# Values of the last tokens once per block, and attention on pairs of heads, in a memory-augmented recurrent layer

## Chip, cores and metric

The kernel runs on one core of a Trainium2 chip. The metric is the device time of one execution in microseconds; the figure for a kernel is the median of its runs.

## What is computed

Two kinds of layer alternate, twice each, on x of 2048 tokens by 512, every one on a layer norm of x and added to it: A, attention with a recurrent memory, and B, a gated MLP whose gate mixes tokens (the change doesn't touch B). A goes through the tokens in 64 segments of 32, one after the other, because the memory of a segment is the output of the one before:

```python
idx = jnp.arange(L)                       # L = 8 memory rows + 32 tokens
mask = (idx[:, None] < M) | (idx[:, None] >= idx[None, :])
for s in range(n_seg):
    h = jnp.concatenate([mem, xs], axis=1)          # 40 rows of 512
    q, k, v = (einsum('btd,dhe->bhte', h, W) for W in (Wq, Wk, Wv))   # 32 heads of 128
    scores = jnp.where(mask, einsum('bhqe,bhke->bhqk', q, k) * scale, -1e9)
    o = einsum('bhqk,bhke->bhqe', softmax(scores), v)
    o = einsum('bhte,hed->btd', o, Wo)
    mem = o[:, :M, :]
    outs.append(o[:, M:, :])
```

Only the first 8 output rows of a segment are needed by the next one. Inputs and outputs are bf16; matrix products accumulate in f32.

## The kernel before

`a_block` (L345) holds the A layer. The weights stay on chip. The matmul helper `mm_chunk` (L394) computes 32 rows of activations times 2048 columns of weights in one pass: 4 contraction steps by 4 column groups of the PE array, 16 matmuls of 512 columns. Since a pass takes 32 rows and a segment has 40, the rows are split. hA is the memory's 8 rows and the first 24 tokens; it must wait for the segment before. hB is the last 8 tokens of each of four segments (a "block" of 128 tokens), which depend on no memory; they fill 32 rows together.

Q and K of hB are computed once per block, in four passes (`bpass`, L456, one per segment at the end of `segment`, L664), turned by DVE into QTB and KTB, and copied by POOL into the last 8 places of QQ and KK (`prep_segment`, L503). V of the last tokens is not: `v_mm` (L544) makes four passes per segment, and in each, column groups 0 and 2 use hA and groups 1 and 3 use hBs, a zero-padded copy of the segment's own 8 rows (L451), so that a head's 40 keys lie together on partitions 0 to 39 (or 64 to 103) of vs.

A segment goes, in PE's order (L596 to L636): four passes for Q and K (each copied from PSUM by ACT, L538, and turned by DVE, L542), half of V's first pass, `scores(0)`, its other half, `denom(0)`, half of V's second pass, `scores(1)`, the other half, `denom(1)`, V's third pass and half of its fourth, `pv(0)`, the rest, the Wo matmuls of half the heads (`wo_pass`, L467), `pv(1)`, a quarter of the Wo matmuls for the last tokens of the block before (`fill_a`, from `y_pass`, L476), the other half of Wo, and the block pass (`fill_b`). `scores` (L554) is two mask matmuls (an identity times the mask, 320 columns) and 16 matmuls, one for each head of the half, in two column groups of the array; ACT's Exp makes E (L565). `denom` (L567) is one matmul with a block of ones, then Ln and Exp on ACT; `probs` (L575) multiplies on DVE. `pv` (L582) has one matmul for each head, two row groups of the array; ACT copies the 8 memory rows into uT (L589), from which Wo is taken at once, and `tok_out` (L592) copies the rest for the next segment's Wo. `build_hA` (L512) puts the memory rows of the Wo product into the next hA: a predicated copy (L515) and a transpose (L516) on DVE, on which the next segment's first matmul waits.

PE, DVE and ACT work in the order of the program (`manual_schedule`, L369). PSUM has four buffers for passes (`acc`), two for scores and denominators (`att`), one of two banks for PV (`attO`). `_consts` (L52) builds the mask with POOL at the start.

Of the kernel before, what the change touches and what calls it, by code (L numbers as in the profile page):

```python
# [14 lines left out]
P = 128  # L15
# [36 lines left out]
def _consts(ctx, tc):  # L52
# [12 lines left out]
    maskf = cp.tile([P, 40], F32, name="maskf")  # L65
    nc.gpsimd.memset(maskf[:], 0.0)
    for g in range(2):
        blk = maskf[64 * g:64 * g + 64, :]
        nc.gpsimd.affine_select(out=blk[:, 8:40], in_=blk[:, 8:40], compare_op=ALU.is_ge, fill=NEG,
                                base=8, pattern=[[1, 32]], channel_multiplier=-1)  # L70
        nc.gpsimd.affine_select(out=blk[:, 0:8], in_=blk[:, 0:8], compare_op=ALU.is_ge, fill=NEG,
                                base=39, pattern=[[0, 8]], channel_multiplier=-1)
    maskN = cp.tile([P, 40], BF16, name="maskN")
# [270 lines left out]
def a_block(tc, c, xd, MV_in, MV_out, mem0, wqkv, Wo, S):  # L344
# [5 lines left out]
    NHA = 8  # L350

    with ExitStack() as ctx:
# [23 lines left out]
        QK_CH = ([0, 1, 4, 5], [2, 3, 6, 7])  # L376

        def chunk_of(j, cg):
            if j < 2:
                return QK_CH[j][cg]  # L380
            if j < 4:
                return 8 + QK_CH[j - 2][cg]
            return 16 + 4 * (j - 4) + cg

        def wcat(cidx):
            return ((Wq_sb, Wk_sb, Wv_sb)[cidx // 8], (cidx % 8) * 512)

        def qk_rhs(j, kt, cg):
            W_sb = Wq_sb if j < 2 else Wk_sb
            return W_sb[:, kt, :].rearrange("p (g2 s2 i eb el) -> p s2 eb g2 i el", g2=2, s2=2, i=8, eb=4)[:, j % 2, cg]  # L390
# [12 lines left out]
        hBs = [pers.tile([P, KT, 32], BF16, name=f"hBs{i}") for i in range(NHA)]  # L403
        NKQ = 3
        KKr = [pers.tile([P, 2, 16, 40], BF16, name=f"KK{i}") for i in range(NKQ)]
        QQr = [pers.tile([P, 2, 16, 40], BF16, name=f"QQ{i}") for i in range(NKQ)]
        uT = [pers.tile([P, H, 32], BF16, name=f"uT{i}") for i in range(2)]
        for t in uT + hBs:
            nc.gpsimd.memset(t[:], 0.0)
# [37 lines left out]
        def ln_turn(tb):  # L447
            hB = blkp.tile([P, KT, 32], BF16, name="hB")
            nc.vector.transpose(out=hB[:].rearrange("p kt r -> p (kt r)"), in_=blk_state[tb].pop("preB")[:])  # L449
            for j4 in range(4):  # L450
                nc.gpsimd.tensor_copy(hBs[(4 * tb + j4) % NHA][:, :, 0:8], hB[:, :, 8 * j4:8 * j4 + 8])  # L451
            KTB = blkp.tile([P, 2, 16, 32], BF16, name="KTB")
            QTB = blkp.tile([P, 2, 16, 32], BF16, name="QTB")
            blk_state[tb].update(hB=hB, KTB=KTB, QTB=QTB)

        def bpass(tb, j):  # L456
            bs = blk_state[tb]
            ps = acc.tile([P, 512], F32, name="psb")
            mm_chunk(ps, lambda kt, cg: bs["hB"][:, kt, :], lambda kt, cg: qk_rhs(j, kt, cg))
            r = rowp.tile([P, 512], BF16, name="rowsB", bufs=2)  # L460
            nc.scalar.copy(r[:], ps[:])  # L461
            nc.vector.transpose(out=bs[("QTB", "KTB")[j // 2]][:, j % 2].rearrange("p a b -> p (a b)"), in_=r[:])  # L462


        HEADS = [16 * g + 8 * half + i for half in range(2) for g in range(2) for i in range(8)]

        def wo_pass(po, lhs, half=None):  # L467
            for n in range(H) if half is None else range(16 * half, 16 * half + 16):
                h = HEADS[n]
                for cg in range(4):  # L470
                    nc.tensor.matmul(po[32 * cg:32 * cg + 32, 0:128], lhsT=lhs[:, h, :], rhs=wo_rhs(h, cg),  # L471
                                     start=(n == 0), stop=(n == H - 1), tile_position=(0, 32 * cg))
                if n % 8 == 7:
                    yield
# [28 lines left out]
        def prep_segment(s):  # L503
            tb, j4 = s // 4, s % 4
            bs = blk_state[tb]
            KK, QQ = KKr[s % NKQ], QQr[s % NKQ]
# [3 lines left out]
            seg_state[s] = dict(KK=KK, QQ=QQ, vs=vs)  # L510
# [12 lines left out]
        def segment(s, fill_a, fill_b):  # L523
            tb, j4 = s // 4, s % 4
            st = seg_state.pop(s)
            KK, QQ, vs = st["KK"], st["QQ"], st["vs"]
            hA_cur, hB_cur = hA[s % 2], hBs[s % NHA]
# [13 lines left out]
            def qk_T(j, r):  # L541
                nc.vector.transpose(out=(QQ, KK)[j // 2][:, j % 2, :, 0:32], in_=r[:])  # L542

            def v_mm(c, kts, ps=None):  # L544
# [6 lines left out]
            def v_out(c, ps):  # L551
                (nc.vector.tensor_copy if c == 3 else nc.scalar.copy)(vs[:, 4 * c:4 * c + 4, :].rearrange("p h e -> p (h e)"), ps[:])  # L552

            def scores(half):  # L554
                psS = att.tile([P, 8, 40], F32, name="psS")
                for g in range(2):
                    nc.tensor.matmul(psS[64 * g:64 * g + 64], lhsT=ident_bf[:, 64 * g:64 * g + 64],
                                     rhs=maskN[:].unsqueeze(1).to_broadcast([P, 8, 40]),
                                     start=True, stop=True, tile_position=(0, 64 * g), skip_group_check=True)
                for hl in range(8):  # L560
                    for g in range(2):
                        nc.tensor.matmul(psS[64 * g:64 * g + 40, hl, :], lhsT=KK[:, half, 8 * g + hl, :], rhs=QQ[:, half, 8 * g + hl, :],
                                         start=False, stop=True, tile_position=(0, 64 * g), skip_group_check=True)
                E[half] = segp.tile([P, 8, 40], BF16, name="E")
                nc.scalar.activation(out=E[half][:], in_=psS[:], func=ACT.Exp, scale=scale)  # L565

            def denom(half):  # L567
                psD = att.tile([P, 8, 40], F32, name="psD")
                nc.tensor.matmul(psD[:], lhsT=ones64[:], rhs=E[half][:], start=True, stop=True)  # L569
                L = segp.tile([P, 8, 40], F32, name="L")  # L570
                nc.scalar.activation(out=L[:], in_=psD[:], func=ACT.Ln)  # L571
                R[half] = segp.tile([P, 8, 40], BF16, name="R")
                nc.scalar.activation(out=R[half][:], in_=L[:], func=ACT.Exp, scale=-1.0)  # L573

            def probs(half):  # L575
                PT[half] = segp.tile([P, 8, 40], BF16, name="PT")
                nc.vector.tensor_tensor(out=PT[half][:], in0=E[half][:], in1=R[half][:], op=ALU.mult)  # L577

            def hview(t, half, lo, hi):
                return t[:].rearrange("p (g s i) r -> p g s i r", g=2, s=2)[:, :, half, :, lo:hi]  # L580

            def pv(half):  # L582
                psO = attO.tile([P, 2, 512], F32, name="psO")
                for hl in range(8):
                    for g in range(2):
                        nc.tensor.matmul(psO[:, g, 40 * hl:40 * hl + 40], lhsT=vs[64 * g:64 * g + 40, 8 * half + hl, :],  # L586
                                         rhs=PT[half][64 * g:64 * g + 40, hl, :], start=True, stop=True)
                ov = psO[:, :, 0:320].rearrange("p g (h q) -> p g h q", q=40)
                nc.scalar.copy(hview(uT_cur, half, 0, 8), ov[:, :, :, 0:8])  # L589
                return ov  # L590

            def tok_out(half, ov):  # L592
                nc.scalar.copy(hview(uT_nxt, half, 8, 32), ov[:, :, :, 8:32])
                nc.vector.tensor_copy(hview(oB, half, 8 * j4, 8 * j4 + 8), ov[:, :, :, 32:40])
# [8 lines left out]
            v0 = v_mm(0, range(0, 2))  # L603
# [5 lines left out]
            v1 = v_mm(1, range(0, 2))  # L609
            scores(1)  # L610
            v_mm(1, range(2, 4), v1)
            denom(1)
            probs(0)
            v_out(1, v1)
            v2 = v_mm(2, range(KT))
            probs(1)
            v_out(2, v2)
            v3 = v_mm(3, range(0, 2))
            ov0 = pv(0)
            v_mm(3, range(2, 4), v3)  # L620
            v_out(3, v3)
# [5 lines left out]
            fill_a()  # L627
            for _ in wo_pass(pw, uT_cur, 1):
# [5 lines left out]
            tok_out(1, ov1)  # L634
            if s + 1 < NSEG:
# [6 lines left out]
        for j in (0, 2, 1, 3):  # L642
            bpass(0, j)
        build_hA(0, None)
        prep_segment(0)
        for s in range(NSEG):
            tb, j4 = s // 4, s % 4
            if j4 == 0:
# [4 lines left out]
                yp = y_pass(tb - 1) if tb > 0 else iter(())  # L653
            if j4 == 1 and tb + 2 < NB:
# [9 lines left out]
            def fill_b():  # L664
                if tb + 1 < NB:
                    bpass(tb + 1, (0, 2, 1, 3)[j4])
# [3 lines left out]
            segment(s, fill_a, fill_b)  # L670
# [44 lines left out]
```

## Time and profile before

| | us |
|---|---|
| median of 3 runs | 2336.5 (2336.31 to 2343.75) |
| profiled execution | 2348.28 |
| span of it, first to last instruction | 2346.5 |
| PE busy | 2018.0 (86%) |
| ACT busy | 1167.1 (50%) |
| DVE busy | 942.5 (40%) |
| POOL busy | 249.8 (11%) |

Busy times are sums over the span, shares are of the span. Matmuls are pipelined, so that the durations of neighbours overlap, and a busy PE is not one at its peak; what a matmul costs in a row of equal ones is the distance between their starts. A PE whose instructions are late is shown as idle with the releaser "issue". The bracket at the end of a timeline row is the idle time of its engine just before it and what ended it.

### The profile page before, as it was taken

Reading aid. Unit: us, or ns where it says so; the run is one execution under the profiler, and the core shown is the slowest. Engines: PE = TensorE matmul, PEld = TensorE weight load, DVE = VectorE, ACT = ScalarE, POOL = GpSimd, SP = SyncE. Lnnn points to the kernel's source line nnn. Section 1 sums busy time; section 2 is a strip of 40 time slices with the busy share of each in tenths; the row PEclk is TensorE's granted clock in tenths of the full one; section 3 lists DMA queues with packets and bytes.
Section 4 is the critical chain, followed back from the end, with each engine's and each line's share of the span. In section 5 each row is a group of like instructions: output and inputs, shape, how many; then the busy total and the mean of one; then the engine's idle time right before and its main releaser. Section 6 shows DMA issues by size and latency. Waiting matters only on the chain. (4 is left out here: it accounts for less than half of the span.)

```text
span 2346.5 us, 108555 instructions
## 1 busy us (share of the span) xinstructions
PE 2018.0 (86%) x50432; PEld 1146.9 (49%) x50432; DVE 942.5 (40%) x2035; ACT 1167.1 (50%) x2660; POOL 249.8 (11%) x567
## 2 busy tenths in 40 slices
PE   0699998999999999781978999999999999996799
PEld 0345544554554454441754545545545555543476
DVE  2444444444444444250334444444444444442422
ACT  0455655655665555470004655655655555663700
POOL 1100100000110100001220000001100000000022
PEclk9999999999999999885989999999999999998899
DMA  9201111111111110229551011111111111102353
GB/s 363 63 20 32 36 36 32 34 34 32 35 33 32 32 37 22 81 69 259 146 178 28 25 33 34 33 32 33 33 34 35 36 32 32 29 22 91 89 121 100
DMA packets 178692, 145.58 MB, mean 62 GB/s; under 512 B 97472, under 2 KB 148288, under 8 KB 175168
## 3 DMA queue, kind: packets, MB, share of 16 engines
q1 hardware_dynamic: 152544, 83.76, 13.1%
q10 hardware_dynamic: 21728, 30.78, 3.8%
q0 software_dynamic: 3968, 24.12, 2.8%
q8 instruction: 394, 6.46, 1.1%
q14 instruction: 58, 0.48, 0.1%
HBM read 88.13 MB, written 33.70 MB: 52 GB/s over the span
## 5 line engine op out<-in xcount | busy, mean ns | idle before, releaser
L399 PEld LDWEIGHTS <-hA 128*32 128x32 bf16 x12288 | 378.4, 96 | 423.3 <-issue 100.7
L399 PE MATMUL psv<-Wv_sb,hA 128*32 128x512 bf16 x4096 | 580.9, 382 | 0.0
L399 PE MATMUL psv<-Wv_sb,hBs 128*32 128x512 bf16 x4096 | 580.7, 382 | 0.0
L538 ACT CAST rows<-psm 128x512 bf16<-128x512 f32 x512 | 303.3, 593 | 103.7 <-PE psm L399 102.2
L471 PE MATMUL pw<-Wo_sb,uT 128*32 128x128 bf16 x16640 | 292.4, 221 | 61.3 <-issue 57.9
L471 PEld LDWEIGHTS <-uT 128*32 128x32 bf16 x16640 | 241.4, 97 | 114.6 <-issue 67.1
L399 PE MATMUL psm<-Wq_sb,hA 128*32 128x512 bf16 x4096 | 276.7, 382 | 9.4 <-DVE hA L516 7.7
L399 PE MATMUL psm<-Wk_sb,hA 128*32 128x512 bf16 x4096 | 272.3, 380 | 0.0
L461 ACT CAST rowsB<-psb 128x512 bf16<-128x512 f32 x128 | 75.0, 586 | 353.7 <-PE psb L399 353.7
L577 DVE TENSOR_TENSOR PT<-E,R 128x320 bf16<-128x320 bf16 x256 | 83.3, 325 | 403.1 <-ACT R L573 403.1
L208 PE MATMUL pg<-wspT,z2n 128*128 128x256 bf16 (+1 forms) x1536 | 175.1, 275 | 57.9 <-DMA wspT<-in_B_w_sp_dram 57.9
L552 ACT CAST vs<-psv 128x512 bf16<-128x512 f32 x384 | 207.8, 575 | 0.0
L208 PEld LDWEIGHTS <-z2n 128*128 128x128 bf16 (+1 forms) x1536 | 150.5, 100 | 82.3 <-issue 65.3
L542 DVE STREAM_TRANSPOSE QQ<-rows 128x512 bf16<-128x512 bf16 x256 | 179.3, 701 | 27.8 <-ACT rows L538 24.2
L542 DVE STREAM_TRANSPOSE KK<-rows 128x512 bf16<-128x512 bf16 x256 | 178.8, 698 | 21.6 <-ACT rows L538 17.8
L509 POOL COPY QQ<-QTB 128x256 bf16<-128x256 bf16 x128 | 56.4, 456 | 1191.8 <-DVE QTB L462 1002.2
L399 PE MATMUL psb<-Wq_sb,hB 128*32 128x512 bf16 x1024 | 73.1, 394 | 103.1 <-DVE hB L449 73.8
L571 ACT ACTIVATE L<-psD 128x320 f32<-128x320 f32 x256 | 112.0, 437 | 98.1 <-PE psD L569 98.1
L515 DVE CAST_PREDICATED pre<-maskM,pw 128x128 bf16<-128x128 uint16 x126 | 36.7, 291 | 306.8 <-PE pw L471 306.8
L399 PEld LDWEIGHTS <-hBs 128*32 128x32 bf16 x4096 | 156.0, 95 | 1.8
L589 ACT CAST uT<-psO 128x128 bf16<-128x128 f32 x256 | 69.9, 273 | 159.9 <-PE psO L586 159.9
L552 DVE CAST vs<-psv 128x512 bf16<-128x512 f32 x128 | 88.6, 692 | 132.9 <-PE psv L399 132.9
(87 smaller groups left out, 2225.7 us busy)
## 6 DMA issues: line engine op xcount, KB each, us to landing
xs<-xd SPq DMA_DIRECT2D x48, 256.0 KB
xs<-xd ACTq DMA_DIRECT2D x48, 256.0 KB
oA_d<-o_sb SPq DMA_DIRECT2D x130, 64.0 KB
xs_y<-xd SPq DMA_DIRECT2D x32, 256.0 KB
xd<-ot_y SPq DMA_DIRECT2D x32, 256.0 KB
Wq_sb<-in_A_Wq_dram POOLq DMA_DIRECT2D x6, 1024.0 KB, 17.8
Wk_sb<-in_A_Wk_dram POOLq DMA_DIRECT2D x6, 1024.0 KB, 26.2
Wv_sb<-in_A_Wv_dram POOLq DMA_DIRECT2D x6, 1024.0 KB, 20.6
```

The lines of the kernel that those rows point to most:

```text
L208: nc.tensor.matmul(pg[0:fsz, :], lhsT=z2n[:, st_i, f0:f0 + fsz], rhs=wspT[:, st_i, :], start=(st_i == 0), stop=(st_i == NT - 1))
L399: nc.tensor.matmul(ps[32 * cg:32 * cg + 32, :], lhsT=lhs(kt, cg), rhs=rhs(kt, cg), start=(kt == 0), stop=(kt == KT - 1), tile_position=(0, ...
L461: nc.scalar.copy(r[:], ps[:])
L471: nc.tensor.matmul(po[32 * cg:32 * cg + 32, 0:128], lhsT=lhs[:, h, :], rhs=wo_rhs(h, cg), start=(n == 0), stop=(n == H - 1), tile_position ...
L509: nc.gpsimd.tensor_copy(QQ[:, :, :, 32:40], bs["QTB"][:, :, :, 8 * j4:8 * j4 + 8])
L515: nc.vector.copy_predicated(out=t[:], mask=maskM[:], data=pw[:, 0:128])
L538: nc.scalar.copy(r[:], ps[:])
L542: nc.vector.transpose(out=(QQ, KK)[j // 2][:, j % 2, :, 0:32], in_=r[:])
L552: (nc.vector.tensor_copy if c == 3 else nc.scalar.copy)(vs[:, 4 * c:4 * c + 4, :].rearrange("p h e -> p (h e)"), ps[:])
L571: nc.scalar.activation(out=L[:], in_=psD[:], func=ACT.Ln)
L577: nc.vector.tensor_tensor(out=PT[half][:], in0=E[half][:], in1=R[half][:], op=ALU.mult)
L589: nc.scalar.copy(hview(uT_cur, half, 0, 8), ov[:, :, :, 0:8])
```

## The change

V of the last tokens is now computed like their Q and K, once per block: VB, in two further passes, r = 0 and 1. The six passes of a block are made by a generator, `b_units`, in twelve halves; a segment takes one ahead of `pv(0)`, one behind it and one at its end. The copies out of PSUM and DVE's transposes of a finished pass are put off to two calls of `flush` in a segment. hBs and the copies of K are dropped: VA and KA hold the 32 rows of hA alone, KTB and VB the 32 last tokens of all four segments of the block, the other three segments' keys masked out.

Heads are taken in pairs. A score matmul's weights are the keys of two heads (64 columns), its moving side the queries of both; the quarters of the product that mix the heads are masked. So a half has 8 matmuls of 80 columns (32 keys of each head's hA, 40 queries) and 8 of 32 columns (32 keys of the block's last tokens, 16 queries: the 8 last and the 8 memory rows), E has 448 columns instead of 320, and PV has 8 matmuls of 80 and 8 of 32 columns that add up in PSUM. Queries are ordered last tokens, memory, first tokens. Since a query's keys now stand in two column ranges, `denom` and `probs` have two instructions where they had one. Heads are spread over passes and partitions in another order, which `qk_rhs` and `wo_pass` follow.

```diff
-        vs = vsp.tile([P, 16, DH], BF16, name="vs")
-        nc.gpsimd.tensor_copy(KK[:, :, :, 32:40], bs["KTB"][:, :, :, 8 * j4:8 * j4 + 8])
-        nc.gpsimd.tensor_copy(QQ[:, :, :, 32:40], bs["QTB"][:, :, :, 8 * j4:8 * j4 + 8])
+        nc.gpsimd.tensor_copy(QQ[:, :, :, 0:8], bs["QTB"][:, :, :, 8 * j4:8 * j4 + 8])
...
+        def b_units(tb):
+            for j in (0, 2, 1, 3, 4, 5):
+                ps = acc.tile([P, 512], F32, name="psb")
+                for kts in (range(0, 2), range(2, 4)):
+                    mm_chunk(ps, lambda kt, cg: bs["hB"][:, kt, :],
+                             lambda kt, cg: qk_rhs(j, kt, cg) if j < 4 else v_rhs(j - 4, kt, cg), kts)
+                    if kts[0] == 0:
+                        yield
+                def out(j=j, ps=ps):
+                    if j >= 4:
+                        nc.scalar.copy(bs["VB"][:, j - 4].rearrange("p i e -> p (i e)"), ps[:])
+                        return
...
+                copies.append(out)
+                yield
...
-                mm_chunk(ps, lambda kt, cg: (hA_cur if cg % 2 == 0 else hB_cur)[:, kt, :],
-                         lambda kt, cg: Wv_sb[:, kt, 2048 * (cg // 2) + 512 * c:2048 * (cg // 2) + 512 * c + 512], kts)
+                mm_chunk(ps, lambda kt, cg: hA_cur[:, kt, :], lambda kt, cg: v_rhs(r, kt, cg), kts)
...
-                                     rhs=maskN[:].unsqueeze(1).to_broadcast([P, 8, 40]),
+                                     rhs=maskN[:, j4, :].unsqueeze(1).to_broadcast([P, 4, 112]),
...
-                for hl in range(8):
-                    for g in range(2):
-                        nc.tensor.matmul(psS[64 * g:64 * g + 40, hl, :], lhsT=KK[:, half, 8 * g + hl, :], rhs=QQ[:, half, 8 * g + hl, :],
+                for i in range(4):
+                    for K, hi, c0 in ((KA, 40, 0), (KTB, 16, 80)):
+                        for g in range(2):
+                            n = 4 * i + 2 * g
+                            nc.tensor.matmul(psS[64 * g:64 * g + 64, i, c0:c0 + 2 * hi],
+                                             lhsT=K[:, r, n:n + 2, :].rearrange("p h k -> p (h k)"), rhs=QQ[:, r, n:n + 2, 0:hi],
...
+                nc.tensor.matmul(psD[:], lhsT=ones64[:], rhs=E[r][:, :, 0:80], start=True, stop=True, skip_group_check=True)
+                nc.tensor.matmul(dB, lhsT=ones64[:], rhs=eB, start=False, stop=True, skip_group_check=True)
...
             scores(0)
             qk_T(3, r3)
-            v_mm(0, range(2, 4), v0)
+            v0 = v_mm(0, range(KT))
             denom(0)
             v_out(0, v0)
             scores(1)
+            probs(0)
+            v1 = v_mm(1, range(KT))
+            v_out(1, v1)
             denom(1)
+            fill_mid()
+            ov0 = pv(0)
+            fill_mid()
             probs(1)
             tok_out(0, ov0)
...
             ov1 = pv(1)
             fill_a()
+            flush()
...
             fill_b()
             store_o(s, pw)
             tok_out(1, ov1)
+            flush()
```

`v_out` is a DVE copy for both passes (before, ACT's for three of four). The mask, [128, 4, 112] with a plane for each segment of a block, is built by 29 POOL instructions where 5 were.

## Rows read from the trace of the kernel before

**Rows 1.** Windows, first attention stage: us; PE, PEld, DVE, ACT, POOL; clock, DMA, GB/s.

```profile
60.00:1014.00 954.00, 857.16 (x24104) 468.15 (x24105) 403.89 (x855) 539.70 (x1246) 85.51 (x219) 0.98 0.13 39
```

**Rows 2.** Tile hA, DVE's transposes in each of the two blocks: durations, first and last start.

```profile
L516 DVE STREAM_TRANSPOSE hA<-pre x64: 270/312/314, 81.2 to 966.7; 128x128 bf16<-128x128 bf16 x64
...
L516 DVE STREAM_TRANSPOSE hA<-pre x64: 269/312/314, 1246.0 to 2131.8; 128x128 bf16<-128x128 bf16 x64
```

**Rows 3.** Timeline of one segment: start us, us, engine, line, operation, out<-in, count.

```profile
459.13 0.31 DVE L516 STREAM_TRANSPOSE hA<-pre 128x128 bf16<-128x128 bf16 x1
459.50 1.05 PE L399 MATMUL psm<-Wq_sb,hA 128*32 128x512 bf16 x16
...
462.10 1.04 PE L399 MATMUL psm<-Wk_sb,hA 128*32 128x512 bf16 x16
...
462.36 0.66 DVE L542 STREAM_TRANSPOSE KK<-rows 128x512 bf16<-128x512 bf16 x1
...
463.50 0.33 PE L557 MATMUL psS<-maskN,ident_bf 128*64 128x320 bf16 x2
...
463.66 0.36 PE L562 MATMUL psS<-QQ,KK 128*40 128x40 bf16 x16
...
464.06 0.44 ACT L565 ACTIVATE E<-psS 128x320 bf16<-128x320 f32 x1 [0.29 <-PE psS L562]
...
464.55 0.30 PE L569 MATMUL psD<-E,ones 128*128 128x320 bf16 x1
...
464.88 0.44 ACT L571 ACTIVATE L<-psD 128x320 f32<-128x320 f32 x1 [0.38 <-PE psD L569]
...
466.69 0.30 PE L569 MATMUL psD<-E,ones 128*128 128x320 bf16 x1 [0.30 <-ACT E L565]
...
468.32 0.43 PE L586 MATMUL psO<-PT,vs 40*128 40x40 bf16 x16
...
468.81 0.28 ACT L589 CAST uT<-psO 128x128 bf16<-128x128 f32 x1
...
469.14 1.08 PE L471 MATMUL pw<-Wo_sb,uT 128*32 128x128 bf16 x64
...
470.29 0.27 PEld L586 LDWEIGHTS <-vs 40*128 40x128 bf16 x16 [0.25 <-DVE oB L594]
470.30 0.37 PE L586 MATMUL psO<-PT,vs 40*128 40x40 bf16 x16
...
471.06 1.07 PE L471 MATMUL pw<-Wo_sb,uT 128*32 128x128 bf16 x64
471.95 1.04 PE L399 MATMUL psb<-Wk_sb,hB 128*32 128x512 bf16 x16
472.18 0.29 DVE L515 CAST_PREDICATED pre<-maskM,pw 128x128 bf16<-128x128 uint16 x1 [1.93 <-PE pw L471]
```

**Rows 4.** Waits of PE, first attention stage: us in total, times, longest.

```profile
PE pw L471 <- issue: 30.4, 28, 3.8
```

**Rows 5.** The page's DMA queues, the one that brings instructions.

```profile
q8 instruction: 394, 6.46, 1.1%
```

**Rows 6.** Lines by form, 500 to 900 us: busy us, mean ns, idle before.

```profile
L538 ACT CAST rows<-psm 128x512 bf16<-128x512 f32 x116 | 68.8, 594 | 20.9 <-PE psm L399 20.7
...
L562 PE MATMUL psS<-QQ,KK 128*40 128x40 bf16 x912 | 20.6, 180 | 0.0
...
L552 DVE CAST vs<-psv 128x512 bf16<-128x512 f32 x28 | 19.4, 692 | 29.1 <-PE psv L399 29.1
...
L577 DVE TENSOR_TENSOR PT<-E,R 128x320 bf16<-128x320 bf16 x56 | 18.2, 325 | 88.2 <-ACT R L573 88.2
```

**Rows 7.** Timeline of POOL at the start, one of four instructions that cut the mask.

```profile
2.39 0.22 POOL L69 TENSOR_SCALAR_AFFINE_SELECT maskf<-maskf 64x32 f32<-64x32 f32 x1
```

**Rows 8.** Late in the first block: timeline of PE, then the window that follows.

```profile
938.60 1.21 PE L399 MATMUL psm<-Wq_sb,hA 128*32 128x512 bf16 x12 [0.74 <-DVE hA L516]
...
938.90:942.30 3.40, 3.40 (x40) 1.38 (x36) 1.00 (x2) 0.90 (x2) 0.00 (x0) 0.50 0.07 19
```

More of the change, by code (lines that the diff above doesn't have):

```diff
@@ L402, in a_block @@
         hA = [pers.tile([P, KT, 32], BF16, name=f"hA{i}") for i in range(2)]
[L403 removed]
         NKQ = 3
[L405 removed]
+        KAr = [pers.tile([P, 2, 16, 32], BF16, name=f"KA{i}") for i in range(2)]
         QQr = [pers.tile([P, 2, 16, 40], BF16, name=f"QQ{i}") for i in range(NKQ)]
         uT = [pers.tile([P, H, 32], BF16, name=f"uT{i}") for i in range(2)]
[L408 removed]
+        for t in uT:
             nc.gpsimd.memset(t[:], 0.0)
@@ L465, in a_block, with flush @@
-        HEADS = [16 * g + 8 * half + i for half in range(2) for g in range(2) for i in range(8)]
+            VB = blkp.tile([P, 2, 4, DH], BF16, name="VB")
+            blk_state[tb].update(hB=hB, KTB=KTB, QTB=QTB, VB=VB)
+        copies, turns = [], []
+        def flush():
+            while turns:
+                turns.pop(0)()
+            while copies:
+                copies.pop(0)()
+        def b_units(tb):
+            bs = blk_state[tb]
+            for j in (0, 2, 1, 3, 4, 5):
[9 more added lines that the diff above has]
+                        return
+                    r = rowp.tile([P, 512], BF16, name="rowsB", bufs=2)
+                    nc.scalar.copy(r[:], ps[:])
+                    turns.append(lambda: nc.vector.transpose(
+                        out=bs[("QTB", "KTB")[j // 2]][:, j % 2].rearrange("p a b -> p (a b)"), in_=r[:]))
+                copies.append(out)
+                yield
@@ L467, in wo_pass @@
         def wo_pass(po, lhs, half=None):
-            for n in range(H) if half is None else range(16 * half, 16 * half + 16):
-                h = HEADS[n]
+            for h in range(H) if half is None else range(16 * half, 16 * half + 16):
+                n = h // 8 * 8 + 2 * (h % 4) + h // 4 % 2
                 for cg in range(4):
-                    nc.tensor.matmul(po[32 * cg:32 * cg + 32, 0:128], lhsT=lhs[:, h, :], rhs=wo_rhs(h, cg),
-                                     start=(n == 0), stop=(n == H - 1), tile_position=(0, 32 * cg))
-                if n % 8 == 7:
+                    nc.tensor.matmul(po[32 * cg:32 * cg + 32, 0:128], lhsT=lhs[:, n, :], rhs=wo_rhs(h, cg),
+                                     start=(h == 0), stop=(h == H - 1), tile_position=(0, 32 * cg))
+                if h % 8 == 7:
@@ L551, in v_out @@
[L551 to L555, printed above, removed]
+                mm_chunk(ps, lambda kt, cg: hA_cur[:, kt, :], lambda kt, cg: v_rhs(r, kt, cg), kts)
+                return ps
+            def v_out(r, ps):
+                nc.vector.tensor_copy(VA[:, r].rearrange("p i e -> p (i e)"), ps[:])
@@ L575, in probs @@
[L575 to L582, printed above, removed]
-                psO = attO.tile([P, 2, 512], F32, name="psO")
[L584 to L589, printed above, removed]
-                return ov
@@ new lines, in probs, with hview, pv @@
+            def probs(r):
+                PT[r] = segp.tile([P, 4, 112], BF16, name="PT")
+                eB, rB = last(E[r], R[r])
+                nc.vector.tensor_tensor(out=PT[r][:, :, 0:80], in0=E[r][:, :, 0:80], in1=R[r][:], op=ALU.mult)
+                nc.vector.tensor_tensor(out=last(PT[r], R[r])[0], in0=eB, in1=rB, op=ALU.mult)
+            def hview(t, r, lo, hi):
+                return t[:].rearrange("p (r g n) q -> p r g n q", r=2, g=2)[:, r, :, :, lo:hi]
+            def pv(r):
+                psO = attO.tile([P, 2, 512], F32, name="psO")
+                for i in range(4):
+                    for V, c0, c1, nq in ((VA, 0, 80, 40), (VB, 80, 112, 16)):
+                        for g in range(2):
+                            o = psO[:, g, 80 * i:80 * i + 80].rearrange("p (s q) -> p s q", s=2)[:, :, 0:nq]
+                            nc.tensor.matmul(o, lhsT=V[64 * g:64 * g + 64, r, i, :],
+                                             rhs=PT[r][64 * g:64 * g + 64, i, c0:c1].rearrange("p (s q) -> p s q", s=2),
+                                             start=(i == 0 and V is VA), stop=True, skip_group_check=True)
+                ov = psO[:, :, 0:320].rearrange("p g (n q) -> p g n q", q=40)
+                nc.scalar.copy(hview(uT_cur, r, 0, 8), ov[:, :, :, 8:16])
+                return ov
@@ L641, in a_block @@
         ln_turn(0)
-        for j in (0, 2, 1, 3):
-            bpass(0, j)
+        for _ in b_units(0):
+            flush()
+        flush()
         build_hA(0, None)
```

108 lines of the change are left out of this document (47 added, 61 removed).

## The prediction, made before the changed kernel ran

> **What bounds the kernel now.** I read the stages first. Columns of the windows view are busy time of PE, weight loads, DVE, ACT, POOL, then the granted clock. In the first attention stage PE is busy for 857 of 954 us, ACT for 540, DVE for 404 and the DMA queues for an eighth, at a granted clock of 0.98 [rows 1]. So PE sets the time there, and the question is what one segment costs it. The transpose that makes the next hA happens 64 times in each block, from 81.2 to 966.7 us and from 1246.0 to 2131.8 [rows 2]: 63 steps of 14.06 us each time. The two blocks' segments are some 1,771 of the 2,346 us of the span, and the diff touches nothing else that repeats.
>
> Next I read one segment in order of time [rows 3]. It starts on PE at 459.50, and its successor at 472.18 + 0.29 + 0.03 + 0.37 = 472.87 (predicated copy, transpose, the same 0.37 us from hA's transpose to the first matmul as at 459.13): 13.37 us with PE waiting only twice, 0.30 us for E before the second denominator and 0.25 us for the oB copy before the second PV. Everything else follows itself: three projection passes from 459.50 to 462.10, 0.867 us each.
>
> The mean of 14.06 is 0.69 above 13.37. The waits put most of it in the Wo matmuls, with "issue" as the releaser: 30.4 us in 28 waits of the first block [rows 4]. PE's instructions arrive by DMA, 394 packets for 6.46 MB [rows 5], so 16 KB or 256 instructions each, some 2.9 packets a segment (374 matmuls and as many weight loads by the code). Where a packet falls on the Wo matmuls, which use up 64 matmuls in about 0.9 us (471.06 to 471.95), the next packet is late. I read the 0.69 us as that.
>
> **The change, part by part**, for one segment:
>
> V. Four passes with alternating hA and hBs become two with hA alone: 2 x 0.867 = **-1.73 us**. The last tokens' V comes back as two more passes a block. The block's passes are then 6, cut into 12 halves, three a segment: two ahead of and behind the first PV, one at the end. Two halves in the middle cost **+0.87**.
>
> The end. Before, a whole pass (471.95 to 472.87) lies beside the chain from the last Wo matmul to the next hA. Now half a pass, 0.43 us, does. The chain keeps its 0.92 us, so PE idles about 0.48 us there and nothing is gained: **0**.
>
> Masks. Each grows from 320 to 448 columns. At 0.867 / (4 x 512) = 0.42 ns a column and two per segment: **+0.11**.
>
> Scores and PV. The counts stay at 16 matmuls each, but half of them stream 80 columns and half 32, where all streamed 40. The 16 scores take 0.36 us and one has a mean of 0.180 [rows 3, 6], so a pair of column groups follows the next by (0.36 - 0.18) / 7 = 26 ns, above the 17 ns that 40 columns need. A floor of 26 and 80 columns at 0.42 ns make 26 and 34 to 36 ns: four pairs longer by 10 ns in each of two scores and two PVs, **+0.16**. Bounds: 0 (the floor hides it) to +0.32 (see the first rival).
>
> Denominators. A second matmul of 128 columns each; one step of the Wo pass, 128 columns in four groups, is 0.89 / 16 = 0.056 us. Two: **+0.11**.
>
> Waits. A whole V pass now stands between the second scores and the second denominator, where half did, so the 0.30 us wait goes: **-0.30**. The oB copy on DVE had to wait for the fourth V's evacuation (0.69 us, [rows 6]) that was queued ahead of it; now both V evacuations are earlier, and the 0.25 us goes: **-0.25**. What is late next is told below. One change of tile shape fewer: the first mask starts at 463.50, where the third projection's end at 462.10 + 0.867 and half a V pass (0.433) make 463.40, so **-0.10**.
>
> Sum: -1.73 + 0.87 + 0.11 + 0.16 + 0.11 - 0.30 - 0.25 - 0.10 = -1.13, so 12.24 us.
>
> **Does the rest keep up?** From the segment's start, with durations from [rows 3, 6]. QK ends at 3.47. The first K's transpose ended at 462.36 + 0.66, or 3.52, and the first product needs it at 3.57 + 0.21 (mask) = 3.78. Scores to 4.12. E, 448 columns instead of 320: 0.44 us becomes 0.55 (the ACT cost of the 512-column cast, 0.594, and of 320, 0.44, lie 0.8 ns a column apart), until 4.78; the denominator comes after the V pass, at 5.15. Second scores 5.43 to 5.98; E behind Ln and Exp until 6.93; second denominator 7.01: slack under 0.1. First PV at 7.85 needs probabilities from 7.0 (two DVE multiplications, at most 0.33 + 0.33 after 6.47) and V by 5.9. The uT copy (468.81, 0.28 us) is done at 8.65 and the Wo matmuls want it at 8.70: slack under 0.1. An open half-done pass holds one PSUM buffer of four across every second segment boundary, and the Wo pass of the last block another; two remain for the QK passes. One is filled in 0.867 us, copied 0.2 us later in 0.59: 1.7 us against two passes, 1.73: slack under 0.1 again. I charge **+0.05** for these three, bounds 0 to +0.4.
>
> ACT loses three V copies and gains half a row copy, DVE gains one V copy and two small products: neither is near its limit in the [rows 1] shares. POOL's copies of K and hB fall away; nobody waited for them. The constants take 24 more POOL instructions of about 0.2 us [rows 7], 5 us under weight loads that last far longer; cost 0, and 5 us if that cover is gone. Two more passes ahead of each block's first segment: up to 2 x 2 x 0.867 = 3.5 us; I take **+2**.
>
> **Instruction supply.** Matmuls per segment fall from 374 to 374 - 32 + 8 + 2 = 352, all from the sparse part; the dense part remains and loses its 0.25 us wait, in which packets could catch up. Stalled segments are about half, so I add half of that and a little less: 0.69 becomes 0.78, **+0.09**; bounds 0.4 to 1.0.
>
> **Clock.** Once in the first block PE fell to half its clock (1.2 GHz) for 3.4 us: 40 matmuls took 3.40 us, where at 2.4 GHz (0.867 / 16 each) they take 2.17: 1.2 us lost [rows 8]. Before it PE had stood in an issue wait in the Wo pass and then 0.74 us for hA with no pass beside it. The change puts a 0.48 us gap into every segment, so I expect a few such stretches: **+4 us** in all, for three.
>
> **Total.** 126 x (-1.13 + 0.05 + 0.09) = -125, with +2 and +4 about **-119 us**. The profiled execution took 2348.28 us, 1.8 more than its span; less 119 is 2229. It lies 11.8 us (0.5%) above the median of the three runs, 2336.5, from which I take the same: **2218 us**, 5.1% less.
>
> **Rivals.**
> (a) *Weight loads pace the block-diagonal matmuls.* Each load of K grows from 40 to 64 columns. If the 26 ns pair step is the load's, it becomes 26 x 64 / 40 = 42 ns for all 8 pairs: 0.33 us against my 0.25, twice a segment, +0.16, +20 us: 2238. Against it: the PV's 16 matmuls, with loads of 128 columns, take the same 0.37 us [rows 3]. Chance 0.14.
> The Trainium skill (TensorE: Matmul & The Clock Gate, LDWEIGHTS) says that a load's time is its columns divided by 1.2, in ns, whatever the rows. By that a 40-column load needs 33 ns, more than the 26 ns measured here, so the trace does not bear it out; 64 columns would need 53 ns and the sum would be near 2270.
> (b) *The attention chain becomes the bound.* The three slacks are under 0.1 us and all from one segment's durations. If they fail together by 0.4 us a segment: 126 x 0.4 = 50, so 2268. For it: DVE and ACT carry irregular work (a block's layer norm, row copies); against it: that work falls outside the tight places. Chance 0.17.
> (c) *Instruction packets catch up in the new gap.* Stalls of 0.4 instead of 0.78: 48 us less, 2170. Against it: the gap lies behind the dense part. Chance 0.08.
> (d) *The clock falls in most segments; slower.* Place: issue wait in Wo, half a pass, hA gap, in one stretch. A fall costs 1.2 us; the gain is 0.99, so from 0.8 falls a segment the kernel is slower, and at one in each 126 x 0.21 = +26, some 2363. For it: the one fall came after just such a pair of idles; against it: 0.98 in a stage with 28 issue waits. Chance 0.07.
> (e) *No change*: (d) at 0.8 falls, or V's saving wholly taken up by (b) at 1 us. Chance 0.03. The saving itself can't fail to occur: 32 matmuls fewer are in the program.
>
> **How the numbers follow.** The forecast keeps 0.51. The range leaves out (c)'s far end, (d) and (e), 0.18 together: 2180 (the bounds of scores and supply at their kind ends, a part of (c)) to 2272 ((a) and (b) whole). A measurement of this kernel tells 0.3% from no change (the runs shown spread by that). Faster by over 0.3%: 0.51 + 0.14 + 0.17 + 0.08 = 0.90; within: 0.03; slower: 0.07.
>
> **What would show it.** Right: hA's transposes 13.1 us apart on average, 12.2 to 12.3 at the best; no wait for oB or E at the PE; a wait of about 0.5 us for hA at each segment; score pairs 26 and 36 ns apart. Wrong: score pairs at 42 ns or more (a); PE waits for ACT's E or uT copies or for PSUM above 0.1 us (b); an issue total per segment far from 0.8 us (c); a granted clock under 0.95 in the attention stages (d).

## The result, and the profile after

The changed kernel takes **2161.8 us** (median of four runs, 2155.1 to 2163.4) where the kernel before takes 2337.7 beside it (2336.3 to 2343.8): a ratio of 0.924 [0.921, 0.926], 176 us less. That is faster than forecast (2218) and below the range, which ended at 2180. The profiled execution took 2162.67 us with a span of 2160.9, so against the 2348.28 and 2346.5 of before it is 185.6 us less; the prediction's sum in that frame was 119. The 67 us between the two are what has to be explained. Some 10 of them may belong to the one execution of before that was profiled: it took 10.5 us more than the median beside it, that of after 0.9 more, where the forecast had carried 11.8 over to both.

First the steps between segments, as in [rows 2]: the transposes that make hA, one row for each block.

```profile
L536 DVE STREAM_TRANSPOSE hA<-pre x64: 269/311/313, 78.8 to 880.3; 128x128 bf16<-128x128 bf16 x64
...
L536 DVE STREAM_TRANSPOSE hA<-pre x64: 270/312/313, 1153.0 to 1949.4; 128x128 bf16<-128x128 bf16 x64
```

The mean step is (880.3 - 78.8) / 63 = 12.72 us and then 12.64, where it was 14.06 twice. The 126 steps took 1771.3 us and now take 1597.9: 173.4 of the 185.6 us. The other 12.2 lie outside them.

Next one segment in order of time (timeline; columns as in [rows 3]). It is one that no late instruction disturbs.

```profile
534.90 0.31 DVE L536 STREAM_TRANSPOSE hA<-pre 128x128 bf16<-128x128 bf16 x1
535.26 1.05 PE L400 MATMUL psm<-Wq_sb,hA 128*32 128x512 bf16 x16 [0.30 <-DVE hA L536]
...
538.83 0.38 PE L579 MATMUL psS<-maskN,ident_bf 128*64 128x448 bf16 x2
539.04 0.20 PE L586 MATMUL psS<-QQ,KA 128*64 128x80 bf16 x2
...
539.28 0.19 PE L586 MATMUL psS<-QQ,KTB 128*64 128x32 bf16 x2
539.39 1.05 PE L400 MATMUL psv<-Wv_sb,hA 128*32 128x512 bf16 x16
...
540.37 0.31 PE L599 MATMUL psD<-E,ones 128*128 128x320 bf16 x1
...
542.21 0.31 PE L599 MATMUL psD<-E,ones 128*128 128x320 bf16 x1
...
543.06 0.21 PE L621 MATMUL psO<-PT,VA 64*128 64x80 bf16 x2
...
543.84 1.07 PE L493 MATMUL pw<-Wo_sb,uT 128*32 128x128 bf16 x64
...
544.84 0.21 PE L621 MATMUL psO<-PT,VA 64*128 64x80 bf16 x2
...
545.63 1.07 PE L493 MATMUL pw<-Wo_sb,uT 128*32 128x128 bf16 x64
...
547.08 0.31 DVE L536 STREAM_TRANSPOSE hA<-pre 128x128 bf16<-128x128 bf16 x1
547.45 0.83 PE L400 MATMUL psm<-Wq_sb,hA 128*32 128x512 bf16 x12 [0.31 <-DVE hA L536]
```

From hA to hA it is 547.08 - 534.90 = **12.18 us**; 12.24 + 0.05 had been forecast, the 0.05 for three narrow places. It also runs as the prediction laid it out from its own start at 535.26: the mask at 3.57 (forecast 3.57), first denominator 5.11 (5.15), second 6.95 (7.01), first PV 7.80 (7.85), Wo 8.58 (8.70). The waits for E and oB are gone, and in their place stands the wait for hA, shown as 0.30 us.

So the clean segment accounts for 1.19 of the 1.38 us. The rest is in the disturbed ones. Mean less clean was 14.06 - 13.37 = 0.69 us; it is now 1597.9 / 126 - 12.18 = 0.50, where 0.78 had been forecast. PE's waits in the first attention stage (60 to 960 us), against [rows 4] (us in total, times, longest):

```profile
PE pw L493 <- issue: 27.3, 25, 3.6
PE psm L400 <- DVE hA L536: 18.5, 56, 0.7
PE pw L493 <- ACT uT L625: 4.9, 8, 1.0
```

The "issue" waits are still there, in the same matmuls, fewer of them: 25 for 28, and in the second stage 19 for 26 (17.5 us for 25.6). This is one, seen in the timeline:

```profile
570.09 0.61 PE L493 MATMUL pw<-Wo_sb,uT 128*32 128x128 bf16 x29
571.69 0.68 PE L493 MATMUL pw<-Wo_sb,uT 128*32 128x128 bf16 x35 [0.99 <-issue]
...
572.74 0.31 DVE L536 STREAM_TRANSPOSE hA<-pre 128x128 bf16<-128x128 bf16 x1
...
573.11 1.05 PE L400 MATMUL psm<-Wq_sb,hA 128*32 128x512 bf16 x16 [0.31 <-DVE hA L536]
```

Between the 29th and the 30th matmul of the segment's last Wo pass PE stands still. From this pass's start to hA it is 572.74 - 570.09 = 2.65 us, against 547.08 - 545.63 = 1.45 in the clean segment: 1.20 us lost to one late packet. The hA wait behind it is no shorter (0.31 us): the gap gives nothing back for a packet that is late in Wo, which is what the prediction held against its rival (c).

Last the clock (windows; columns as in [rows 1]):

```profile
60.00:1014.00 954.00, 821.04 (x22943) 461.31 (x22950) 499.64 (x1108) 522.53 (x1162) 54.14 (x95) 0.96 0.18 55
...
60.00:880.00 820.00, 756.96 (x22072) 423.17 (x22072) 462.00 (x1015) 469.60 (x1056) 44.75 (x80) 1.00 0.12 36
...
1140.00:1950.00 810.00, 759.54 (x22074) 425.41 (x22074) 457.88 (x1005) 466.52 (x1055) 42.46 (x78) 0.99 0.12 34
...
1406.50:1409.90 3.40, 3.40 (x40) 1.36 (x36) 1.22 (x3) 1.34 (x3) 0.37 (x1) 0.50 0.13 34
```

The first window is that of [rows 1] and now runs past the stage's end; where the segments run the granted clock is 1.00 and 0.99. Of the three more half-clock stretches for which I had put 4 us none came: the segments have a single one, the last window (40 matmuls in 3.40 us, as in [rows 8]), and before they had two, at 938.9 and 1932.2 us. Here too PE had stood before it, for 1.49 us in an issue wait in Wo and 0.31 us for hA; but issue waits of that kind come in 39 segments, and the clock fell in one.

### The profile page after: what moved, and what is told of

It is laid out like the page before. It is cut to its first block, busy times and chain, and to the rows that moved or that the text cites. A ratio compares the mean times of both kernels' runs of the same rounds, so it can differ in the third digit from the quotient of the medians.

```text
span 2160.9 us, 102768 instructions
## 1 busy us (share of the span) xinstructions
PE 1865.7 (86%) x47588; PEld 1090.1 (50%) x47616; DVE 1087.1 (50%) x2419; ACT 1054.1 (49%) x2340; POOL 179.7 (8%) x319
## 5 line engine op out<-in xcount | busy, mean ns | idle before, releaser
L400 PEld LDWEIGHTS <-hA 128*32 128x32 bf16 x12288 | 302.7, 96 | 349.4 <-DVE hA L536 93.2
L400 PE MATMUL psv<-Wv_sb,hA 128*32 128x512 bf16 x4096 | 268.0, 382 | 0.0
L564 DVE STREAM_TRANSPOSE KA<-rows 128x512 bf16<-128x512 bf16 x256 | 182.1, 711 | 36.2 <-ACT rows L560 36.0
L573 DVE CAST VA<-psv 128x512 bf16<-128x512 f32 x256 | 177.0, 691 | 43.5 <-PE psv L400 27.6
L400 PE MATMUL psb<-Wq_sb,hB 128*32 128x512 bf16 x1024 | 80.7, 393 | 92.2 <-DVE hB L449 72.4
L529 POOL COPY QQ<-QTB 128x256 bf16<-128x256 bf16 x128 | 49.4, 402 | 1211.3 <-PE psO L621 839.7
L222 DVE TENSOR_TENSOR gb<-pg,bsp_bc 128x256 f32<-128x256 f32 x96 | 40.6, 423 | 208.1 <-PE pg L219 208.1
L590 ACT ACTIVATE E<-psS 128x448 bf16<-128x448 f32 x256 | 136.8, 534 | 0.0
L540 ACT COPY o_sb<-pw 128x128 f32<-128x128 f32 x130 | 34.5, 265 | 194.2 <-DVE pre L535 181.6
L400 PEld LDWEIGHTS <-hB 128*32 128x32 bf16 x3072 | 57.1, 96 | 140.8 <-DVE hB L449 72.4
```

Of the source, the lines that this page charges most:

```text
L222: nc.vector.tensor_tensor(out=gb[0:fsz, :], in0=pg[0:fsz, :], in1=bsp_bc[0:fsz, t0:t0 + TC2], op=ALU.add)
L400: nc.tensor.matmul(ps[32 * cg:32 * cg + 32, :], lhsT=lhs(kt, cg), rhs=rhs(kt, cg), start=(kt == 0), stop=(kt == KT - 1), tile_position=(0, ...
L529: nc.gpsimd.tensor_copy(QQ[:, :, :, 0:8], bs["QTB"][:, :, :, 8 * j4:8 * j4 + 8])
L564: nc.vector.transpose(out=QQ[:, j % 2, :, 8:40] if j < 2 else KA[:, j % 2], in_=r[:])
L573: nc.vector.tensor_copy(VA[:, r].rearrange("p i e -> p (i e)"), ps[:])
L590: nc.scalar.activation(out=E[r][:], in_=psS[:], func=ACT.Exp, scale=scale)
```

## Experiments

The open question was what sets the 0.5 and 0.69 us. Counting PE's instructions (each matmul, each weight load and the few semaphores) from one late packet to the next gives multiples of 256, so it can be told for every segment at which of its own instructions a packet ends. Worked out so from the two traces, for segments of the same length, by the place of the packet's end (modulo 256, counted from the first QK weight load; 112 segments in all; the first 15 instructions of the second half of Wo before and the first 28 after stand by themselves):

```
place                          before: segments, mean excess   after: segments, mean excess
second half of Wo, its start              6, 0.00 us                     18, 0.16 us
second half of Wo, the rest              50, 1.19                        39, 1.23
around the segment's start               18, 0.80                        20, 0.39
QK passes behind it                      30, 0.16                         9, 0.17
other places                              8, 0.00                        26, 0.07
```

The packed traces hold the packets too, each with the time at which it landed. Every issue wait of over 0.6 us in Wo within the segments, 52 before and 39 after, ends at instruction 449 or 450 + 256 j of PE's stream, where j is the number of the packet that landed last, 1.20 to 1.59 us before: PE stands at the first instruction of the packet that it waits for. No packet in the segments is used sooner than 1.20 us after it landed (360 packets before, 337 after).

This is the theory **P**: the place decides. A packet that ends in the second half of Wo, past its start, costs 1.2 us in either kernel, and a segment's count of PE instructions against 256 decides how often that happens: 749 before, 19 less than three packets, so the place creeps by 19 a segment; 704 or 705 after, 64 less, so it all but returns every fourth segment. Its rival **R** says that the place does not matter and more or fewer instructions, or a gap, set the excess. To tell them apart I added small matmuls ("pads", 40 columns into a spare PSUM tile) that bring a segment to a whole number of packets, with a few more once ahead of each block to choose the place. The edits are shown shortened.

**1 and 2. After, 32 pads a segment behind the last pass, 10 or 43 ahead of the first block.**

```diff
+        def pad(n):
+            px = att.tile([P, 4, 112], F32, name="psX")
+            for k in range(n):
+                cg = k % 4
+                nc.tensor.matmul(px[32*cg:32*cg+32, 0, 0:40], lhsT=ones64[:, 32*cg:32*cg+32], rhs=maskN[:, 0, 0:40], ...)
...
             fill_b()
+            pad(32)
             store_o(s, pw)
...
+        pad((10, 108)[block])      # the second kernel: (43, 108)
         build_hA(0, None)
```

> The changed kernel with 32 small matmuls (and their 32 weight loads) more per segment, in the gap before the next hA: 768 PE instructions a segment, three packets of 256, so that packets meet every segment at the same place; 10 of the same matmuls ahead of block 1 and 108 ahead of block 2 choose the place. Theory P (a late packet costs 1.2 us where it falls in the second half of the Wo matmuls and nearly nothing elsewhere): nearly all segments at 12.2 us, mean below 12.3, about 2162 - 0.45 x 126 = 2105 us, although PE has 9% more instructions. Rival R (the stalls became fewer because there are fewer instructions and a gap in which packets catch up): more instructions in that gap bring more stalls, mean 12.7 to 13.0, 2160 to 2200 us.

> As e1_lock_good, with 43 small matmuls instead of 10 ahead of block 1: the same work in every segment, the packets 66 instructions earlier against it, so that a boundary falls in the second half of the Wo matmuls in every segment. Theory P: nearly every segment at 13.3 to 13.5 us, about 2162 + 0.7 x 126 = 2250 us. Rival R: the same time as e1_lock_good within 10 us.

Measured: 2195.6 (ratio to before 0.935 [0.930, 0.940]) and 2254.8 (0.959 [0.955, 0.964]), mean steps of 12.95 and 12.92, then 13.40 and 13.42. The second is what P said. The first missed P's forecast and lies in R's range; PE's waits in the first stage show that the packet's end, meant for a harmless place, fell among the pads, right behind Wo.

```profile
PE psX L529 <- issue: 52.6, 58, 1.4
```

Still, the two programs differ in 33 matmuls ahead of one block and the shift of place that these make, and are 59 us apart.

**3 and 8. Before, 9 pads a segment; 90 or 27 ahead of the second block.** Pads stand behind the pass that covers hA's chain.

```diff
             fill_b()
+            pad(9)
             store_o(s, pw)
...
+        pad((12, 90)[block])       # the second kernel: (12, 27)
         build_hA(0, None)
```

> The kernel before with 9 small matmuls more per segment behind the block pass (766 PE instructions instead of 748, and about 1.3 others), 12 ahead of block 1 and 90 ahead of block 2. Theory P: most segments at 13.4 to 13.5 us, the 0.69 us of stalls gone, about 2337 - 0.6 x 126 = 2261 us. Then of the change's 176 us about 150 are its work (13.37 to 12.18 us a segment). Rival R: the added matmuls cost their 0.1 to 0.2 us a segment, 2337 + 13 to 25 = 2350 to 2362 us.

> e3_before_lock with 27 small matmuls instead of 90 ahead of block 2, nothing else. In e3_before_lock block 1 went at 13.37 us a segment and block 2 at 14.5, with a packet boundary in the Wo matmuls of every segment. Theory P: block 2 at 13.4 to 13.5 us as well, 2343 - 126/2 x 1.0 = 2280 us, within 15. Rival R: no difference from e3_before_lock, 2335 to 2350 us.

Measured: 2342.7 (0.997 [0.995, 0.999]) and **2277.7** (0.974 [0.971, 0.976]). In the third kernel the 90 pads put the second block at a bad place, the 12 the first at a good one; the eighth kernel has a good one in both. The steps of hA, third kernel, then the eighth:

```profile
L525 DVE STREAM_TRANSPOSE hA<-pre x64: 269/312/315, 80.2 to 931.0; 128x128 bf16<-128x128 bf16 x64
...
L525 DVE STREAM_TRANSPOSE hA<-pre x64: 269/311/314, 1207.2 to 2122.6; 128x128 bf16<-128x128 bf16 x64
```

```profile
L525 DVE STREAM_TRANSPOSE hA<-pre x64: 269/312/314, 81.5 to 931.8; 128x128 bf16<-128x128 bf16 x64
...
L525 DVE STREAM_TRANSPOSE hA<-pre x64: 269/311/314, 1208.7 to 2058.0; 128x128 bf16<-128x128 bf16 x64
```

And PE's waits from 1200 to 2130 us, third kernel, then the eighth:

```profile
PE pw L471 <- issue: 48.8, 44, 1.6
```

```profile
PE pw L471 <- issue: 5.5, 4, 3.7
```

The second block's step is 14.53 us in the one and 13.48 in the other, with the same instructions in each segment. In the eighth most segments take the clean 13.37 (91 of 126). So the place alone is worth 65 us in the kernel of before, 2.8%. R, by which the place doesn't matter, has no room for this. The third kernel's total missed both forecasts, since only its first block had the place that was meant.

**4. After, with the second half pass moved from the middle to the end**, so that PE does not wait for hA.

```diff
             ov0 = pv(0)
-            fill_mid()
             probs(1)
...
+            fill_mid()
             fill_b()
             store_o(s, pw)
```

> The changed kernel with the half pass behind the first PV moved to the segment's end, beside the chain to the next hA: a whole pass there as before, the gap of 0.48 us filled, the same instructions. If the gap were an idle time that only the pass's place costs, a segment without stalls would fall by 0.44 us to 11.75 (about 2107 us). My reading of the timeline: the Wo matmuls then wait for the uT copy, which stands behind Ln and Exp on ACT, by about 0.35 to 0.4 us, so 12.1 to 12.2 us, and the stalls rise a little (0.50 to 0.6) since the gap no longer takes them up: 2155 to 2170 us.

Measured: 2171.2 (0.924 [0.920, 0.928], the ratio of the changed kernel); the clean segment is 12.19. The gap is closed, and a new wait takes its place, in the first stage:

```profile
PE pw L493 <- ACT uT L625: 26.7, 68, 1.0
```

By the same count as above a packet that ends around the segment's start costs 0.76 us here, as before the change (0.80), and 0.39 with the gap. So the gap does take in half of that lateness, and nothing of it in Wo (1.38 us here).

**5. After, reordered**: the first PV right behind the second denominator, the half passes behind it and at the end, the uT copy ahead of the second Exp on ACT, the oB copy ahead of the probabilities on DVE.

```diff
-            denom(1)
-            fill_mid()
+            rec1 = denom(1)        # its Exp is issued later
             ov0 = pv(0)
+            rec1()
             fill_mid()
-            probs(1)
             tok_out(0, ov0)
+            probs(1)
...
+            fill_mid()
             fill_b()
             store_o(s, pw)
```

> The changed kernel with both half passes of the middle moved: the first PV follows the second denominator at once, one half pass stands behind it and a whole pass at the segment's end, and on ACT the copy into uT goes ahead of the second half's last Exp, DVE's oB copy ahead of the second probabilities. If what held e4_end_pass up is the uT copy behind Ln and Exp, the segment without stalls falls by the 0.44 us of the half pass, from 12.18 to 11.75 us, and the total to 2105 to 2125 us. If the attention chain (E, Ln, Exp, probabilities of the second half) is as long as it is read, the second PV or the first waits instead and the segment stays at 12.0 to 12.2: 2140 to 2170 us.

Measured: 2138.1 (0.915 [0.911, 0.918]), clean segment 12.02, mean steps of 12.44 and 12.56 (in the profiled execution, which took 2154.9). The wait for uT goes; one of 0.2 us for the second probabilities stays in every segment:

```profile
PE psO L623 <- DVE PT L611: 14.2, 64, 0.2
```

**6 and 7. The reordered kernel with 32 pads at the end (98 and 108 ahead), and kernel 1 with 90 ahead of the first block.**

> e5_reorder with 32 small matmuls a segment at its end, 98 ahead of block 1 and 108 ahead of block 2, so that packets meet each segment at the same place. There is no gap now that hides the small matmuls: 0.3 to 0.45 us a segment. Theory P: stalls of 0.5 us go, and the sum is 0.05 to 0.2 us a segment less than e5_reorder, 6 to 25 us; if the place is a bad one, up to 100 us more.

> e1_lock_good with 90 small matmuls instead of 10 ahead of block 1, nothing else. In e1_lock_good the boundary of a packet fell among the small matmuls themselves, right behind the Wo matmuls, and cost 0.4 to 1.2 us a segment; 160 instructions further the boundaries fall in the first QK pass, in the first PV and in the last tokens' Wo matmuls, where the changed kernel shows waits of 0 to 0.3 us. Theory P: mean 12.2 to 12.4 us a segment, 2105 to 2130 us, against 2196 and 2255 for the same work in e1 and e2. Rival R (more instructions, more stalls): 2160 to 2200 us.

Measured: 2205.7 (0.942 [0.940, 0.944]) with steps of 13.15 and 12.91, and 2205.2 (0.942 [0.939, 0.945]) with 12.99 and 13.01. P failed as I had drawn it: with 32 quick pads behind the quick Wo no place tried was free. The first is P's bad place (up to 100 us more than kernel 5); the second fits neither forecast. In kernel 7 the late packets show as many short waits, 19 in Wo (6.6 us) and 29 in the QK passes behind the pads (9.3 us) between 100 and 880 us. My reading: the place matters by how quickly PE uses up instructions around it, and the pads had lengthened the quick stretch.

**9 and 11. After, 8 pads behind each of the four QK passes instead; 68 or 80 ahead of the first block.** PE takes 0.867 us for a pass of 32 instructions there, so the pads are not in a quick stretch.

```diff
             r0 = qk(0)
+            pad(8)
             r2 = qk(2)
+            pad(8)
             qk_T(0, r0)
             r1 = qk(1)
+            pad(8)
             qk_T(2, r2)
             r3 = qk(3)
+            pad(8)
...
+        pad((68, 108)[block])      # the second kernel: (80, 108)
         build_hA(0, None)
```

> The changed kernel with 768 PE instructions a segment again, but the 32 small matmuls stand eight each behind the four Q and K passes, where PE uses instructions slowly, and not behind the Wo matmuls; 68 ahead of block 1 and 108 ahead of block 2. In e1 and e7 the small matmuls made the quick stretch of Wo longer, and e7 paid 0.8 us a segment wherever the boundary fell. Theory P, narrowed (a packet is late when the 256 instructions in front of it are used up quickly; the place of the boundary decides): most segments alike at 12.18 + 0.2 to 0.4 for the small matmuls, mean 12.4 to 12.6, 2120 to 2150 us. Rival R (three packets a segment cost more than 2.75, wherever): mean above 12.7, 2165 to 2210 us, as in e1 and e7.

> e9_lock_sparse with 80 small matmuls instead of 68 ahead of block 1, nothing else. In e9 the last ten segments of both blocks went at 12.38 us each, without a late packet, once the slow drift (half an instruction a segment) had brought the boundary to the 44th instruction or less of the last tokens' Wo matmuls; 24 instructions further the boundary is there from the first segments on. Theory P: nearly all segments at 12.38, mean 12.40 to 12.45, 2178 - 0.33 x 126 = 2136 us, 2130 to 2145, under the changed kernel's 2162 in spite of 9% more PE instructions. Rival R: as e9, 2165 to 2185 us.

Measured: 2178.4 (0.930 [0.927, 0.932]) and **2136.2** (0.911 [0.910, 0.912]). Kernel 9 lies in R's range. Its place moved by half an instruction in each segment, and only late segments of each block (ten in a row in the first) had a flat 12.38 us; kernel 11 starts where these stood. Its steps of hA and its waits in the first stage:

```profile
L545 DVE STREAM_TRANSPOSE hA<-pre x64: 270/311/313, 79.8 to 864.7; 128x128 bf16<-128x128 bf16 x64
...
L545 DVE STREAM_TRANSPOSE hA<-pre x64: 269/311/313, 1134.3 to 1918.1; 128x128 bf16<-128x128 bf16 x64
```

```profile
PE psm L400 <- DVE hA L545: 20.9, 63, 0.7
PE pw L493 <- issue: 5.9, 3, 3.6
```

The steps are 12.46 and 12.44, and the pads cost 0.20 us of that (clean 12.38 against 12.18). Of after's 25 issue waits in the memory's Wo 3 are left. Twelve matmuls, once, ahead of a block are worth 42 us; the two kernels ran in different rounds, with the kernel before at 2344.6 and 2343.2 beside them.

**10 and 12. The reordered kernel with such pads: 32 a segment, 73 ahead; 31 a segment, 99 and 138 ahead.**

> e5_reorder with the same small matmuls behind the Q and K passes, 73 ahead of block 1 and 108 ahead of block 2. Theory P, narrowed: most segments at 12.02 + 0.2 to 0.4, mean 12.25 to 12.45, 2100 to 2135 us, under the 2138 of e5_reorder. Rival R: 2150 us and more.

> e10_reorder_sparse with 31 small matmuls a segment instead of 32, so that the drift is half an instruction instead of one and a half, and 99 and 138 ahead of the blocks. In e10 segments 11 to 31 of block 1 went at 12.22 us. Theory P: nearly all segments there, mean 12.22 to 12.35, 2158 - 0.35 x 126 = 2114 us, 2105 to 2125, under the 2138 of e5_reorder. Rival R: as e10, 2150 us and more.

Measured: 2158.3 (0.921 [0.919, 0.923]), again what R gave, and **2117.6** (0.904 [0.902, 0.907]), what P gave. In kernel 10 the place drifted by 1.5 instructions a segment and out of the good stretch: 12.43 in the first block, 12.78 in the second. One pad fewer a segment and another start give 12.32 and 12.33:

```profile
L545 DVE STREAM_TRANSPOSE hA<-pre x64: 270/311/313, 79.6 to 856.1; 128x128 bf16<-128x128 bf16 x64
...
L545 DVE STREAM_TRANSPOSE hA<-pre x64: 269/311/313, 1124.6 to 1901.1; 128x128 bf16<-128x128 bf16 x64
```

This kernel beats both kernels of the case: it takes 9.6% less than before, and 44 us less than after.

Of P's forecasts of a time, those for kernels 2, 8, 11 and 12 came in, 6 fell in its bad case, and those for 1, 3, 7, 9 and 10 missed; R's came in for 1, 9 and 10. So P doesn't tell beforehand which place is good: the pads had to be moved until one was. That the place decides rests on the pairs, 3 and 8, 9 and 11, and on the packets in the traces.

Not tried: the two halves of the change apart. The block's V, computed once, has keys of four segments and needs the masks and the pairs of heads that come with it.

## Why the prediction was wrong in size

Direction and the mechanism of the saving held; the time fell out of the range by 18 us. Point by point, in the profiled frame (-185.6 against -119; the runs' medians are 176 apart):

- **The work of a segment** (V, masks, scores and PV, denominators, waits, the end). Forecast 13.37 - 1.13 + 0.05 = 12.29, measured 12.18: 126 x 0.11 = 14 us of the miss. 0.05 of the 0.11 is the charge for the narrow places. Score pairs follow each other by (539.28 - 539.04) / 7 = 34 ns on average, 35 behind 80 columns and 29 to 33 behind 32, where I had 36 and 26; that part of the sum was right to 0.03 us. Rival (a), 42 ns a pair, fell. By the Trainium skill (TensorE: Matmul & The Clock Gate, LDWEIGHTS) a load of 64 columns takes 53 ns, an estimate from its columns divided by 1.2; with pairs 34 ns apart the trace does not agree. The 2270 us that the prediction had by it come to 2262 by its own terms.
- **"Does the rest keep up?"** The three narrow places held but for 8 waits for uT in the first stage (4.9 us). Rival (b) fell. Kernel 4 shows how near it was: half a pass moved, and that wait was there 68 times, for 26.7 us.
- **The failing step is "Instruction supply"**: "the dense part remains and loses its 0.25 us wait, in which packets could catch up", so 0.69 becomes 0.78. Measured 0.50, so that the term +0.09 should have been -0.19: 126 x 0.28 = 35 us, half of the miss. I had taken the excess for a matter of how dense the work is. It is one of where a packet ends as well: the late packet costs the same 1.2 us after as before, but 39 of the 112 segments of one length pay it where 50 did. Packets don't end less often in that half of Wo (57 segments after, 56 before); after, 18 of them end in its start, where they cost 0.16 us, before 6. Were the segments spread evenly over the 256 places, 44 and 49 would pay. So half of the fall is that the costly stretch of places is shorter, for a reason that no run shows, and half how 704 and 749 happen to fall on 256, which nobody chose. Kernels 3 and 8, and 9 and 11, show with all else equal that the place decides. A smaller part is the segment's start, where a packet's end costs 0.39 for 0.80, and 0.76 again in kernel 4 without the gap for hA. Of the 17 us of excess that the 112 segments lost, Wo has 12 and the start 7; at the other places the excess rose by 1.
- **Rival (c)** had the catching-up in the new gap at 0.4. It came nearest to the time, for a third by its own reason (the start's 7 us of 17), and the range cut it off at 2180. With the place unknown, its whole span, from the 0.1 us of kernel 8 to the 1.2 of kernel 3's second block, belonged in the range.
- **Clock** (+4) and **startup** (+2) did not come: the segments have one half-clock stretch where before had two, and outside the 126 steps, where these 6 us stand in the sum, the span fell by 12.2 us. That is 18 us of the miss. The first hA is 2.4 us earlier, the stretch between the blocks 6.6 us shorter (279.3 to 272.7), the end 3.2. Some 2.5 of these should be the last segments of the two blocks, which have no successor (1.19 each); the rest is not settled.

14 + 35 + 18 = 67.

## What to carry to other kernels

Read the undisturbed step of a loop and its mean apart: the first follows from the work and could be forecast to 1%, the second holds a term that depends on how the count of PE instructions in a step falls on packets of 256, and on how quickly PE uses up the packet ahead. Give that term bounds as wide as from nothing to one late packet in every step, or settle it by a few pads. Put pads where PE is slow, not behind a quick stretch, and check that the place stays put over the loop.

## What was unexpected in the hardware

- A program's length ahead of a loop changes the loop's time: 27 matmuls or 90 ahead of the second block make its step 13.48 or 14.53 us.
- More instructions can be faster. Kernel 11 fetches 406 packets of instructions where after fetches 372, and takes 26 us less. The page's instruction queue, for after and then for kernel 11:

```profile
q8 instruction: 372, 6.09, 1.1%
```

```profile
q8 instruction: 406, 6.65, 1.3%
```

- A late packet costs 1.2 us in the second half of Wo and close to nothing in places where PE is slow. The traces tell why it is the second half and not the first. For the waits in Wo, a packet's transfer began 0.2 to 2.1 us after PE had begun the packet ahead of it, took 0.9 to 1.9 us, and its first instruction followed 1.2 to 1.6 us later: 2.9 to 4.4 us in all, 3.3 in the median. In the clean segments PE uses up the 256 instructions that end in the second half of Wo in 2.0 to 2.5 us, for they hold the first half, the second PV and the last tokens' Wo, and those that end in the first half in 3.9 to 7.0 us. What sets the start of a transfer no run isolates, nor why the first instructions of the second half go nearly free.
